# Two decode attentions on one core: the small input first, a memset in pieces, and a last weight load in shrinking parts

## Chip, cores and metric

The kernel runs on one core of one Trainium2 chip. The metric is the device time of one execution in microseconds (us), median over runs. The span in a profile (first to last instruction) is 1.7 to 2.2 us shorter than the time of the same run.

## The reference, cut to what matters

Two independent one-token attentions, A and B, with 32 query heads, 16 key/value heads, head size 128, model width 576. A looks at the last 2048 cache rows, B at all 8192. All data are bf16.

```python
q = (x @ wq).reshape(...)                 # x: 576 numbers, wq: 576 x 4096
p = softmax((q @ k.T) * 128**-0.5)        # per head
y = (p @ v).reshape(4096) @ wo            # wo: 4096 x 576
# the result is concat(y_A, y_B)
```

About 103 MB must come from HBM, and each byte is used once.

## The kernel before

A small scheduler takes operations with the tiles they read and write, derives the semaphore waits and emits one program per engine. SyncE ("sp") issues all big loads into six 2 MB slots, reused in turn. These parts matter here:

```python
def setup(pool):                       # GpSimd zeroes small tiles, among them xpad
    ...
for b in range(2):                     # then the two halves of ptm, 32 KB per partition each
    add("pool", lambda pool, b=b: pool.memset(ptm[:, b, :].bitcast(U32), 0), writes=[("ptm", b)])

def setup2(pool):                      # four more memsets, without a wait between them
    pool.memset(identf[:], 0.0); pool.memset(pick[:], 0.0)
    pool.memset(same[:], 0.0);   return pool.memset(opj[:], 0.0)
# ... then affine_selects, each of which waits for the memset of its tile

add("act", lambda act: act.activation(warm[:, 4:8], warm[:, 0:4], ACT.Exp), ...)
load_x(0); load_x(1)                   # on ACT: 128 runs of 10 bytes each, after the activation

def x_columns(P):                      # VectorE: two tiny tensor_scalars, x into xpad
    for e in range(2):
        add("dve", lambda dve, e=e: dve.tensor_scalar(xpad[:, P, 5*e:5*e+5, 0], xtwo[:, P, 0:5],
                                                      par[2][:, e:e+1], None, ALU.mult), ...)
# the q projection (TensorE, "PE") needs xpad and wq; its end frees the slots of wq

def load_wo(P, k):                     # wo in three loads: 14, 14 and 4 rows per partition
    lo, hi = k * WO_SLOT, min(HQ, (k + 1) * WO_SLOT)
    ...
def wo_part(P, k, s):                  # four matmuls a row; waits for its whole load
    ...
for k in range(3):                     # the last work of the kernel
    wo_part(1, k, load_wo(1, k))
finish_out(1); store_out(1)            # copy of PSUM, store
```

A "row" of wo is 1,152 bytes in each of the 128 partitions. wo has 32 of them.

Of the kernel before, what the change touches and what calls it, by code (L numbers as in the profile page):

```python
# [6 lines left out]
U32 = mybir.dt.uint32  # L7
# [4 lines left out]
HQ = 32  # L12
HKV = 16
DH = 128
DM = 576
# [4 lines left out]
NSLOT = 6  # L20
# [1 line left out]
TS = 64  # L22
WQ_UNITS = 9
WQ_SLOT = 4
WO_SLOT = 14
OUTW = DM // 4


# [9 lines left out]
class Program:  # L38
# [11 lines left out]
        self.dma_sems = {}  # L50
        self.dma_count = {}

    def add(self, eng, fn, reads=(), writes=(), dma=None):
        op = Op(eng, fn, tuple(reads), tuple(writes), dma)
        deps = []
        for r in op.reads:
            w = self.writer.get(r)
            if w is not None:
                deps.append((w, True))
            if r[0] == "bank":  # L60
                deps += [(o, False) for o in self.readers.get(r, ())]
        for r in op.writes:
            w = self.writer.get(r)
            if w is not None:
                deps.append((w, False))
            deps += [(o, False) for o in self.readers.get(r, ())]
        for r in op.reads:
            self.readers.setdefault(r, []).append(op)
        for r in op.writes:
            self.writer[r] = op  # L70
            self.readers[r] = []
        for o, raw in deps:
            if o is op:
                continue
            if o.dma_sem is None and o.eng == eng and (not raw or eng in ("pe", "sp")):
                continue
            op.deps.append(o)
            o.needed = True
        if dma is not None:
            if dma not in self.dma_sems:  # L80
                self.dma_sems[dma] = self.nc.alloc_semaphore("dma_" + dma)
                self.dma_count[dma] = 0
            self.dma_count[dma] += 16
            op.value = self.dma_count[dma]
        self.ops.append(op)
        return op
# [50 lines left out]
def bass_concat_heads__sliding_block_cached__gqa_block_cached__decode_kernel(  # L137
# [13 lines left out]
    xs = [A_x, B_x]  # L151
# [3 lines left out]
    wos = [A_wo, B_wo]  # L155
# [14 lines left out]
    add = prog.add  # L170

    slots = nc.alloc_sbuf_tensor("slots", [128, NSLOT, SLOT], BF16)
    kt = nc.alloc_sbuf_tensor("kt", [128, NKT, UNIT], BF16)
    ptm = nc.alloc_sbuf_tensor("ptm", [128, 2, 32 * 512], BF16)
# [8 lines left out]
    xtwo = nc.alloc_sbuf_tensor("xtwo", [128, 2, 8], BF16)  # L183
# [6 lines left out]
    opj = nc.alloc_sbuf_tensor("opj", [128, 2, 64], BF16)  # L190
# [11 lines left out]
    B_M = ("bank", 7)  # L202


    def setup(pool):
        def zero(t):
            return pool.memset(t, 0.0)
        zero(ident[:])
        zero(xpad[:])
        zero(selq[:])  # L210
        pool.memset(onesf[:], 1.0)
        zero(warm[:])
        return zero(qtm[:])

    add("pool", setup, writes=["ident", ("xpad", 0), ("xpad", 1), "selq", "ones", "warm", ("qtm", 0), ("qtm", 1)])

    def select(t, base_, pattern, mult):
        return lambda pool: pool.affine_select(out=t, in_=t, compare_op=ALU.not_equal, fill=1.0,
                                               base=base_, pattern=pattern, channel_multiplier=mult)

    add("pool", select(ident[:], 0, [[-1, 128]], 1), reads=["ident"], writes=["ident"])
    add("pool", select(selq[:], 0, [[-32, 4]], 1), reads=["selq"], writes=["selq"])
    for b in range(2):
        add("pool", lambda pool, b=b: pool.memset(ptm[:, b, :].bitcast(U32), 0), writes=[("ptm", b)])  # L224

    def setup2(pool):
        pool.memset(identf[:], 0.0)
# [11 lines left out]
    for n in (2, 4):  # L239
        add("dve", lambda dve, n=n: dve.tensor_reduce(par[n][:, :], ident[:, :].rearrange("p (m g) -> p g m", g=n),  # L240
                                                      AX.X, ALU.add),
            reads=["ident"], writes=[("par", n)])
# [4 lines left out]
    slot_n = [0]  # L247

    def load(src_of, view_of, what):
        s = slot_n[0] % NSLOT  # L250
        slot_n[0] += 1
        res = ("slot", s)
        add("sp", lambda sp: sp.dma_start(view_of(slots[:, s, :]), src_of()), writes=[res], dma="slot%d" % s)
        return s


    def load_x(P):
        def go(act):
            x = xs[P]
            with nc.allow_non_contiguous_dma(reason="small x load"):  # L260
                src = bass.AP(tensor=x.tensor, offset=x.offset, ap=[[9, 64], [4, 2], [1, 5]])
                return act.dma_start(xtwo[:, P, 0:5], src)
        add("act", go, writes=[("xtwo", P)], dma="x%d" % P)

    def load_wq(P, k):
        lo, hi = k * WQ_SLOT * 2048, min(WQ_UNITS, (k + 1) * WQ_SLOT) * 2048
        return load(lambda: wqs[P].rearrange("(m r) n -> m (r n)", m=64)
                    .rearrange("m (e y) -> (m e) y", e=2)[:, lo:hi],
                    lambda v: v[:, 0:hi - lo], "wq")
# [6 lines left out]
            return a[0, i * G[P]:(i + 1) * G[P], r0:r0 + CH[P], :].rearrange("g (p t) d -> p g (t d)", t=TS)  # L276
        return load(src, lambda v: v, "kv")

    def load_wo(P, k):
        lo, hi = k * WO_SLOT, min(HQ, (k + 1) * WO_SLOT)  # L280
        return load(lambda: wos[P].rearrange("(p j) n -> p (j n)", p=128)[:, lo * DM:hi * DM],
                    lambda v: v[:, 0:(hi - lo) * DM], "wo")


    def x_columns(P):
# [188 lines left out]
    def combine(P):  # L474
        n = NCH[P]
        last = n - 1
        d = 2
        add("dve", lambda dve: dve.tensor_scalar(acc[:, d, :], opsum[:, 0:DH], st(P, C_AL + last), None, ALU.mult),  # L478
            reads=[B_O, ("st", P, C_AL)], writes=[("acc", d)])
        for c in range(last):  # L480
            add("dve", lambda dve, c=c: dve.scalar_tensor_tensor(acc[:, d, :], acc[:, c, :], st(P, C_AL + c),
                                                                 acc[:, d, :], ALU.mult, ALU.add),
                reads=[("acc", c), ("acc", d), ("st", P, C_AL)], writes=[("acc", d)])

        def mm(pe):
            for r in range(4):
                ins = pe.matmul(misc[:, 0:32], lhsT=pick[:, r, :], rhs=acc[:, d, 32 * r:32 * r + 32],
                                start=(r == 0), stop=(r == 3))
            return ins
        add("pe", mm, reads=["pick", ("acc", d)], writes=[B_M])  # L490
        add("dve", lambda dve: dve.tensor_copy(opj[:, P, 0:32], misc[:, 0:32]), reads=[B_M], writes=[("opj", P)])

    def wo_part(P, k, s):
        lo, hi = k * WO_SLOT, min(HQ, (k + 1) * WO_SLOT)

        def mm(pe):
            for jj in range(lo, hi):
                for j in range(4):
                    o = (jj - lo) * DM + j * OUTW
                    ins = pe.matmul(misc[32 * j:32 * j + 32, 0:OUTW], lhsT=opj[:, P, jj:jj + 32],  # L500
                                    rhs=slots[:, s, o:o + OUTW], start=(jj == 0), stop=(jj == HQ - 1))
            return ins
        add("pe", mm, reads=[("opj", P), ("slot", s)], writes=[B_M])

    def finish_out(P):
        add("dve", lambda dve: dve.tensor_copy(outsb[:, P, :], misc[:, 0:OUTW]), reads=[B_M], writes=[("outsb", P)])
# [5 lines left out]
            return eng.dma_start(dst, src)  # L512
        add("sp", put, reads=[("outsb", P)], writes=[("out", P)], dma="out%d" % P)


    load_x(0)
    load_x(1)

    def k_phase(P, c, between):
        pend = None  # L520
# [39 lines left out]
    n = 64 * NS[0]  # L560
# [12 lines left out]
    v_keep(1, 0)  # L573
    softmax_transpose(1, 1, pb1)
    weights(1)
    for k in range(3):
        wo_part(0, k, load_wo(0, k))
    finish_out(0)
    vb1 = list(range(NS[1]))
    v_some(1, 1, vb1, NS[1])  # L580
    store_out(0)
    combine(1)
    for k in range(3):
        wo_part(1, k, load_wo(1, k))
    finish_out(1)
    store_out(1)
    add("sp", lambda sp: sp.nop(), reads=[("out", 0), ("out", 1)])
# [29 lines left out]
```

## Time and profile before

| kernel before | |
|---|---|
| time, median | 254.84 us (254.61 to 255.10, 4 runs) |
| span of the profiled run | 252.8 us |
| moved by DMA | 103.24 MB |
| first packet of a big load | 1.74 us |
| last landing of wo of B | 249.30 us |
| end of PE's last matmul | 250.30 us |

First the page of the kernel before: the span in 40 slices of 6.3 us. A digit is the busy share in tenths, and GB/s is what the DMA engines moved.

```profile
PE   0018999787799995888694994858943634332563
DMA  7999999999999999999999999999999999999960
GB/s 283 398 440 430 433 415 428 433 417 425 432 423 423 430 423 423 433 421 423 430 417 436 425 415 436 430 412 441 421 421 419 430 425 425 428 423 429 425 284 31
```

The DMA engines are full from the second slice to the last two; PE is full only here and there. 103.24 MB at 425 GB/s take 243 us. Only what lies before the first packet and after the engines begin to run dry can change the time.

Next its chain of waits, with start, length and what was waited for. Two stretches matter, the head and the tail:

```profile
2.54 9.25 DMA xtwo<-in_A_x_dram
11.79 0.03 issue
11.81 6.05 DVE xpad L287 x2
...
219.21 28.70 DMA slots<-in_B_wo_dram
247.91 0.04 issue
247.95 2.38 PE misc L500 x60
```

The head waits 9.25 us for 1.2 KB of x, then 6.05 us for two VectorE operations on 5 elements per partition. The timeline of the kernel before (start, length, engine, line, operation) shows what GpSimd (POOL) did meanwhile:

```profile
3.12 13.79 POOL L224 MEMSET ptm<- 128x8192 uint32 x2
...
17.61 0.21 POOL L230 MEMSET opj<- 128x128 bf16 x1
17.96 0.29 POOL L218 TENSOR_SCALAR_AFFINE_SELECT identf<-identf 128x128 f32<-128x128 f32 x1
```

And this is the timeline of the tail before:

```profile
243.44 1.87 PE L500 MATMUL misc<-slots,opj 128*32 128x144 bf16 x56 [0.37 <-DVE opj L491]
247.95 2.35 PE L500 MATMUL misc<-slots,opj 128*32 128x144 bf16 x72 [2.64 <-DMA slots<-in_B_wo_dram]
250.36 0.31 DVE L506 CAST outsb<-misc 128x144 bf16<-128x144 f32 x1 [7.06 <-PE misc L500]
```

PE waits for a whole 14-row load, and then has 72 matmuls (18 rows) to do at the very end. They ran at a granted TensorE clock (the share of full speed that the throttle allowed) of 0.50, 33 ns each.

One more reading comes from the landing records. Each load has sixteen landing records, read here as one for each of the sixteen DMA engines. For the last load of the kernel before these landings are, in us:

```
242.83 242.84 242.90 243.00 243.05 243.43 243.71 244.14 | 247.35 247.37 247.42 247.46 247.56 247.63 249.06 249.30
```

Eight engines are done 3 to 6.5 us before the other eight. PE starts on a load only after its sixteenth landing (at 247.95 us after a last landing at 247.91), so the slowest engine sets the end.

### The profile page before, as it was taken

How to read it: one execution, taken by the hardware profiler on the slowest of the kernel's cores; microseconds unless marked ns; L12 is line 12 of the kernel's file. 1: busy time of each engine (PE TensorE's matmuls, PEld its weight loads, DVE VectorE, ACT ScalarE, POOL GpSimd, SP SyncE). 2: the span in 40 equal slices, each digit the busy share in tenths (PEclk: the TensorE clock that was granted, in tenths of full speed). 3: DMA queues.
4: the chain of work that ended last, by engine and by line, in shares of the span. 5: the costliest groups of instructions: out<-in, count | busy, mean ns of one | idle time of the engine just before them, and what ended most of it. 6: DMA issues, size and time to landing. Idle time of an engine off the chain costs nothing.

```text
span 252.8 us, 7319 instructions
## 1 busy us (share of the span) xinstructions
PE 167.1 (66%) x3438; PEld 131.7 (52%) x3438; DVE 79.3 (31%) x141; ACT 87.3 (35%) x92; POOL 22.4 (9%) x31
## 2 busy tenths in 40 slices
PE   0018999787799995888694994858943634332563
PEld 0003877456578874766474673655732633232453
DVE  0181545427544462357341340313425100000010
ACT  2000766445566683565461461423630000000000
POOL 8996000000000000000000000000000000000000
PEclk9999999999979999799997798968977665555555
DMA  7999999999999999999999999999999999999960
GB/s 283 398 440 430 433 415 428 433 417 425 432 423 423 430 423 423 433 421 423 430 417 436 425 415 436 430 412 441 421 421 419 430 425 425 428 423 429 425 284 31
DMA packets 7822, 103.24 MB, mean 408 GB/s; under 512 B 1136, under 2 KB 1136, under 8 KB 1648
## 3 DMA queue, kind: packets, MB, share of 16 engines
q1 hardware_dynamic: 7504, 102.77, 96.1%
q8 instruction: 27, 0.44, 0.7%
q10 hardware_dynamic: 288, 0.00, 0.1%
q14 instruction: 3, 0.02, 0.0%
HBM read 102.76 MB, written 0.00 MB: 407 GB/s over the span
## 4 chain that ended last, share of the span: by engine, by line
DMA 53%; PE 38%; DVE 6%; issue 1%; POOL 1%; ACT 0%; SPq 0%; POOLq 0%
DMA slots<-in_B_k_cache_dram 21%; PE ktps L339 20%; DMA slots<-in_B_v_cache_dram 17%; DMA slots<-in_B_wo_dram 11%; PE sacc L362 7%; DMA xtwo<-in_A_x_dram 4%; PE opsum L464 3%; DVE xpad L287 3%; PE opsum L302 2%; PE misc L302 2%; PE misc L500 2%; DVE ptm L407 1%; PE misc L396 1%; PE misc L444 1%; PE misc L431 0%
## 5 line engine op out<-in xcount | busy, mean ns | idle before, releaser
L345 ACT ACTIVATE kt<-ktps 128x1024 bf16<-128x1024 bf16 x80 | 78.0, 1023 | 65.3 <-PE ktps L339 65.1
L339 PE MATMUL ktps<-ident,slots 128*128 128x128 bf16 x1280 | 86.4, 231 | 19.1 <-DMA slots<-in_B_k_cache_dram 19.1
L339 PEld LDWEIGHTS ktps<-ident,slots 128*128 128x128 bf16 x1280 | 80.0, 105 | 31.5 <-DMA slots<-in_B_k_cache_dram 20.3
L348 DVE COPY kt<-ktps 128x1024 bf16<-128x1024 bf16 x80 | 55.3, 691 | 79.2 <-PE ktps L339 79.0
L464 PE MATMUL opsum<-slots,ptm 128*32 128x128 bf16 x1280 | 28.3, 256 | 29.4 <-DMA slots<-in_B_v_cache_dram 28.9
L464 PEld LDWEIGHTS opsum<-slots,ptm 128*32 128x32 bf16 x1280 | 24.5, 116 | 35.6 <-DMA slots<-in_B_v_cache_dram 33.0
L362 PE MATMUL sacc<-kt,qtm 128*32 128x512 bf16 (+1 forms) x384 | 30.1, 411 | 0.3 <-DVE kt L348 0.3
L302 PE MATMUL opsum<-slots,xpad 128*32 128x512 bf16 x72 | 8.7, 460 | 19.3 <-DVE xpad L287 19.3
L302 PEld LDWEIGHTS opsum<-slots,xpad 128*32 128x32 bf16 x72 | 2.5, 112 | 22.2 <-issue 21.3
L224 POOL MEMSET ptm<- 128x8192 uint32 x2 | 13.8, 6926 | 0.0
L478 DVE TENSOR_SCALAR acc<-opsum,stat 128x128 f32<-128x128 f32 x2 | 0.7, 346 | 39.6 <-PE opsum L464 39.6
L362 PEld LDWEIGHTS sacc<-kt,qtm 128*32 128x32 bf16 x384 | 7.0, 98 | 6.9 <-ACT kt L345 1.1
L500 PE MATMUL misc<-slots,opj 128*32 128x144 bf16 x256 | 8.1, 323 | 3.4 <-DMA slots<-in_B_wo_dram 2.6
L308 ACT ACTIVATE qrow<-opsum 128x512 bf16<-128x512 f32 x2 | 1.2, 597 | 24.1 <-PE misc L302 24.1
L500 PEld LDWEIGHTS misc<-slots,opj 128*32 128x32 bf16 x256 | 7.4, 146 | 3.8 <-DMA slots<-in_B_wo_dram 3.4
L287 DVE TENSOR_SCALAR xpad<-xtwo,par 128x5 bf16<-128x5 bf16 x4 | 6.4, 3098 | 8.3 <-DMA xtwo<-in_A_x_dram 8.3
L302 PE MATMUL misc<-slots,xpad 128*32 128x512 bf16 x72 | 8.5, 450 | 0.0
L385 ACT ACTIVATE psb<-sacc,stat 128x2048 bf16<-128x2048 f32 x3 | 5.9, 1967 | 7.5 <-DVE stat L379 7.5
L562 POOL MEMSET ptm<- 128x512 uint32 x1 | 0.5, 526 | 86.1 <-PE opsum L464 86.1
L407 DVE TENSOR_SCALAR ptm<-misc,par 128x256 bf16<-128x256 bf16 (+1 forms) x16 | 6.9, 526 | 3.7 <-PE misc L396 3.7
L396 PE MATMUL misc<-ident,psb 128*128 128x128 bf16 x48 | 4.1, 235 | 3.7 <-DVE ptm L407 3.7
L396 PEld LDWEIGHTS misc<-ident,psb 128*128 128x128 bf16 x48 | 3.0, 105 | 5.4 <-DVE ptm L407 4.3
(50 smaller groups left out, 37.2 us busy)
## 6 DMA issues: line engine op xcount, KB each, us to landing
slots<-in_B_k_cache_dram SPq DMA_DIRECT2D x16, 2048.0 KB, 22.3
slots<-in_B_v_cache_dram SPq DMA_DIRECT2D x16, 2048.0 KB, 25.1
slots<-in_A_k_cache_dram SPq DMA_DIRECT2D x4, 2048.0 KB, 19.3
slots<-in_A_v_cache_dram SPq DMA_DIRECT2D x4, 2048.0 KB, 20.7
slots<-in_A_wq_dram SPq DMA_DIRECT2D x2, 2048.0 KB, 9.6
slots<-in_B_wq_dram SPq DMA_DIRECT2D x2, 2048.0 KB, 18.6
slots<-in_A_wo_dram SPq DMA_DIRECT2D x2, 2016.0 KB, 25.0
slots<-in_B_wo_dram SPq DMA_DIRECT2D x2, 2016.0 KB, 28.7
```

The lines of the kernel that those rows point to most:

```text
L224: add("pool", lambda pool, b=b: pool.memset(ptm[:, b, :].bitcast(U32), 0), writes=[("ptm", b)])
L287: add("dve", lambda dve, e=e: dve.tensor_scalar(xpad[:, P, 5 * e:5 * e + 5, 0], xtwo[:, P, 0:5], par[2][:, e:e + 1], None, ALU.mult), read ...
L302: ins = pe.matmul(qps[c][32 * j:32 * j + 32, :], lhsT=xpad[:, P, x, :], rhs=slots[:, s, o:o + 512], start=(u == 0), stop=(u == WQ_UNITS - 1))
L339: ins = pe.matmul(ktps_bf[q][:, t * 128:(t + 1) * 128], lhsT=slots[:, s, o:o + 128], rhs=ident[:, :], start=True, stop=True, is_transpose= ...
L345: add("act", lambda act, q=q, dst=dst: act.activation(dst, ktps_bf[q], ACT.Copy), reads=[("bank", q)], writes=[("kt", u, q)])
L348: add("dve", lambda dve, q=q, dst=dst: dve.tensor_copy(dst, ktps_bf[q]), reads=[("bank", q)], writes=[("kt", u, q)])
L362: ins = pe.matmul(sacc[32 * j:32 * j + 32, o:o + w], lhsT=qtm[:, P, g * 32:(g + 1) * 32], rhs=rhs, start=(g == 0 and o % 512 == 0), stop=( ...
L385: return act.activation(psb[:, 0:w * G[P]].rearrange("p (x g) -> p x g", g=G[P]), src, ACT.Exp, bias=st(P, C_NB + c), scale=SCALE, accum_o ...
L396: ins = pe.matmul(misc_bf[:, t * 128:(t + 1) * 128], lhsT=psb[:, o:o + 128], rhs=ident[:, :], start=True, stop=True, is_transpose=True)
L407: ins = dve.tensor_scalar(dst, src, par[G[P]][:, e:e + 1], None, ALU.mult)
L464: ins = pe.matmul(opsum[32 * j:32 * j + 32, 0:DH], lhsT=ptm[:, pb, o:o + 32], rhs=slots[:, s, b * 128:(b + 1) * 128], start=(i == 0 and u ...
L500: ins = pe.matmul(misc[32 * j:32 * j + 32, 0:OUTW], lhsT=opj[:, P, jj:jj + 32], rhs=slots[:, s, o:o + OUTW], start=(jj == 0), stop=(jj == ...
```

## The change

The intent: let x arrive before the big loads, let VectorE in between the pieces of the memset, and give PE less to do after the last bytes arrive.

```diff
+    load_x(0)                      # now first in ACT's program
+    load_x(1)
     def setup(pool):
...
     for b in range(2):
-        add("pool", lambda pool, b=b: pool.memset(ptm[:, b, :].bitcast(U32), 0), writes=[("ptm", b)])
+        for h in range(8):
+            add("pool", lambda pool, b=b, h=h: pool.memset(ptm[:, b, h * 2048:(h + 1) * 2048].bitcast(U32), 0),
+                writes=[("ptm", b)])
...
-    def load_wo(P, k):             # one load for one slot
+    def load_wo(P, lo, parts):     # one slot, several loads, a semaphore for each part
...
-    for k in range(3):
-        wo_part(1, k, load_wo(1, k))
+    for lo, parts in ((0, [14]), (14, [8, 4]), (26, [3, 2, 1])):
+        for made in load_wo(1, lo, parts):
+            wo_part(1, *made)
```

wo of A keeps its loads of 14, 14 and 4 rows.

More of the change, by code (lines that the diff above doesn't have):

```diff
@@ L24 @@
 WQ_SLOT = 4
-WO_SLOT = 14
 OUTW = DM // 4
@@ L51, in __init__, with add @@
         self.dma_count = {}
-    def add(self, eng, fn, reads=(), writes=(), dma=None):
+    def add(self, eng, fn, reads=(), writes=(), dma=None, after=()):
         op = Op(eng, fn, tuple(reads), tuple(writes), dma)
@@ L61, in add @@
                 deps += [(o, False) for o in self.readers.get(r, ())]
+        for r in after:
+            deps += [(o, False) for o in self.readers.get(r, ())]
         for r in op.writes:
@@ L202, in bass_concat_heads__sliding_block_cached__gqa_block_cached__decode_kernel, with load_x, go @@
     B_M = ("bank", 7)
+    def load_x(P):
+        def go(act):
+            x = xs[P]
+            with nc.allow_non_contiguous_dma(reason="small x load"):
+                src = bass.AP(tensor=x.tensor, offset=x.offset, ap=[[9, 64], [4, 2], [1, 5]])
+                return act.dma_start(xtwo[:, P, 0:5], src)
+        add("act", go, writes=[("xtwo", P)], dma="x%d" % P)
+    load_x(0)
+    load_x(1)
     def setup(pool):
@@ L254, in load @@
         return s
-    def load_x(P):
-        def go(act):
-            x = xs[P]
-            with nc.allow_non_contiguous_dma(reason="small x load"):
-                src = bass.AP(tensor=x.tensor, offset=x.offset, ap=[[9, 64], [4, 2], [1, 5]])
-                return act.dma_start(xtwo[:, P, 0:5], src)
-        add("act", go, writes=[("xtwo", P)], dma="x%d" % P)
     def load_wq(P, k):
@@ L277, in load_kv, with go @@
         return load(src, lambda v: v, "kv")
-    def load_wo(P, k):
-        lo, hi = k * WO_SLOT, min(HQ, (k + 1) * WO_SLOT)
-        return load(lambda: wos[P].rearrange("(p j) n -> p (j n)", p=128)[:, lo * DM:hi * DM],
-                    lambda v: v[:, 0:(hi - lo) * DM], "wo")
+    def load_wo(P, lo, parts):
+        s = slot_n[0] % NSLOT
+        slot_n[0] += 1
+        o, made = 0, []
+        for k, rows in enumerate(parts):
+            n = rows * DM
+            res = ("slot", s) if len(parts) == 1 else ("slot", s, k)
+            def go(sp, lo=lo, n=n, o=o):
+                return sp.dma_start(slots[:, s, o:o + n],
+                                    wos[P].rearrange("(p j) n -> p (j n)", p=128)[:, lo * DM:lo * DM + n])
+            add("sp", go, writes=[res], after=[("slot", s)], dma="slot%d" % s if res == ("slot", s) else "part%d_%d" % (s, k))
+            made.append((lo, lo + rows, s, o, res))
+            lo += rows
+            o += n
+        return made
     def x_columns(P):
@@ L491, in combine, with wo_part @@
         add("dve", lambda dve: dve.tensor_copy(opj[:, P, 0:32], misc[:, 0:32]), reads=[B_M], writes=[("opj", P)])
-    def wo_part(P, k, s):
-        lo, hi = k * WO_SLOT, min(HQ, (k + 1) * WO_SLOT)
+    def wo_part(P, lo, hi, s, o0, res):
         def mm(pe):
@@ L498, in mm @@
                 for j in range(4):
-                    o = (jj - lo) * DM + j * OUTW
+                    o = o0 + (jj - lo) * DM + j * OUTW
                     ins = pe.matmul(misc[32 * j:32 * j + 32, 0:OUTW], lhsT=opj[:, P, jj:jj + 32],
@@ L502, in mm @@
             return ins
-        add("pe", mm, reads=[("opj", P), ("slot", s)], writes=[B_M])
+        add("pe", mm, reads=[("opj", P), res], writes=[B_M])
     def finish_out(P):
@@ L513, in store_out @@
         add("sp", put, reads=[("outsb", P)], writes=[("out", P)], dma="out%d" % P)
-    load_x(0)
-    load_x(1)
     def k_phase(P, c, between):
@@ L575, in bass_concat_heads__sliding_block_cached__gqa_block_cached__decode_kernel @@
     weights(1)
-    for k in range(3):
-        wo_part(0, k, load_wo(0, k))
+    for lo, parts in ((0, [14]), (14, [14]), (28, [4])):
+        for made in load_wo(0, lo, parts):
+            wo_part(0, *made)
     finish_out(0)
@@ L582, in bass_concat_heads__sliding_block_cached__gqa_block_cached__decode_kernel @@
     combine(1)
-    for k in range(3):
-        wo_part(1, k, load_wo(1, k))
+    for lo, parts in ((0, [14]), (14, [8, 4]), (26, [3, 2, 1])):
+        for made in load_wo(1, lo, parts):
+            wo_part(1, *made)
     finish_out(1)
```

## The prediction

One sentence of the recorded text is cut where the mark stands. The 0.9 us are my estimate from the 6.93 us of the memset, and rest on the idea that VectorE's wait ends with one GpSimd instruction. The trace before did not show that: the wait ended at 17.86 us, and the memset at 16.91.

> What bounds the kernel now. The DMA engines, from 2 us to the end. The page's DMA row is 9 in all slices but the first and the last two; 103.24 MB at about 425 GB/s are 243 us of the 252.8 us span. The single packet records agree: between 2 and 242 us about 16.1 packets are in flight on 16 engines, without a gap. PE (66%), ACT and DVE have slack. Only the head (first packet at 1.7 us) and the tail can give anything back.
>
> The head. The chain of waits starts with the x load: issued at 2.54 us behind the first ACTIVATE, landed at 11.79. Its first packet moves at 6.65 us, when the first wq load's eight packets per engine are through, and then one small packet passes per 0.61 us wq packet. Then the two tensor_scalars into xpad take 6.03 us; the same ones for B take 0.23. They end when the second ptm memset (6.93 us, until 16.9) is over. [...] With memsets of about 0.9 us (an eighth of 6.93, plus start-up) DVE should wait 0.9 us or less, and an early x should land at 3 to 7 us. The q projection then begins when wq lands, near 8 us, instead of 18.0, and ends near 16.5 instead of 24.4. That frees about 8 us of PE time, but not on the limiting path: loads of 10.5 MB (25 us) are queued at 4 us, and the fourth K slot, issued at 21.7, kept the queue full. I expect about 0 from it. One risk: ACT and SP now both issue at 0.73 us, and an x issue takes 0.59; the whole stream may start up to 0.5 us later.
>
> The tail. The engines don't finish together. Of B's second wo load the first engine is done at 241.4, the last at 247.91; of the third, 242.8 and 249.30. Each instruction fetch (16 KB, about 1.05 us) sets one engine back by about 1.5 us. Bytes and PE instructions stay, so this skew stays. Now PE waits until 247.95 for 14 rows, then runs 72 matmuls (18 rows) in 2.35 us, to 250.3; a row costs 0.13 us of PE and 0.345 us of the slowest engine. With 8, 4, 3, 2, 1 rows PE follows the arrivals and has one row left after the last landing. Extra: 24 packets per engine at about 8 ns (16,128 B take 604 ns, 4,608 B take 178) and three completions of 9 ns: 0.2 us. So last landing 249.5, PE end about 249.9 (one row plus some 0.3 us of latency) instead of 250.3. Copy and store stay.
>
> Sum: -0.4 us in the tail, 0 from the head, up to +0.5 at risk at the start: 254.5 us, range 253.5 to 255.4. Chances: faster by over 2% 0.01, within 2% 0.98, slower 0.01.
>
> Shown right by: q matmuls starting near 8 us, xpad ops under 1 us each; DMA row full as before; fourth K issue near 10 us; last wo landing 249.3 to 249.7; after it 4 to 12 matmuls. Shown wrong by: x landing after 11 us; first wq packet later than 2 us; the last landing moved by over 0.5 us.
>
> What would make it wrong: instruction fetches falling on other engines (1.5 us either way), dearer small packets, or a stream at another rate when PE is 8 us ahead.

## The result

| | before | after |
|---|---|---|
| time, median | 254.84 us (4 runs) | 254.60 us (254.14 to 254.81, 4 runs) |
| ratio to before | | 0.9988 (0.9971 to 1.0005) |
| x of A issued, landed | 2.54, 11.79 us | 0.73, 10.66 us |
| xpad operations end | 17.86 us | 18.41 us |
| fourth K load of A issued | 21.71 us | 21.92 us |
| last landing of wo of B | 249.30 us | 249.18 us |
| PE's last matmul ends | 250.30 us | 249.47 us |

A ratio is the mean time of one kernel's fast runs over that of the other's in the same rounds, so it is not quite the ratio of the medians. The difference is not clear of noise: the interval holds 1.

The page of after, the same rows:

```profile
PE   0008999787799995888893784956934535333573
DMA  7999999999999999999999999999999999999971
GB/s 273 400 450 418 431 431 407 433 431 423 420 434 423 421 434 418 423 434 420 423 431 426 418 431 429 423 418 439 423 422 423 428 423 429 426 426 425 415 309 56
```

The DMA row is as full as before. The head in the chain of waits of after:

```profile
0.73 9.93 DMA xtwo<-in_A_x_dram
10.68 7.74 DVE xpad L306 x2
```

The issue moved up by 1.8 us, but the landing only by 1.1. The two VectorE operations take longer than before. The timeline of after says why:

```profile
0.73 0.59 ACTq L211 DMA_DIRECT2D xtwo<-in_A_x_dram  x1
0.73 1.33 SPq L268 DMA_DIRECT2D slots<-in_A_wq_dram  x3
...
3.12 14.35 POOL L238 MEMSET ptm<- 128x1024 uint32 x16
...
18.16 0.20 POOL L245 MEMSET opj<- 128x128 bf16 x1
18.51 0.29 POOL L231 TENSOR_SCALAR_AFFINE_SELECT identf<-identf 128x128 f32<-128x128 f32 x1
```

ACT and SyncE issue in the same instant. The sixteen memset pieces run back to back: in their single records each starts about 0.06 us before the one ahead of it ends. When x lands, eight of them and four more memsets are still to end. VectorE finishes at 18.41 us, in the first gap of GpSimd (18.37 to 18.51). Before it was the same: it finished at 17.86, in the gap from 17.82 to 17.96, and not when the ptm memset ended at 16.91.

The tail of after:

```profile
245.68 1.10 PE L517 MATMUL misc<-slots,opj 128*32 128x144 bf16 x32 [0.60 <-DMA slots<-in_B_wo_dram]
247.09 0.43 PE L517 MATMUL misc<-slots,opj 128*32 128x144 bf16 x16 [0.30 <-DMA slots<-in_B_wo_dram]
248.16 0.37 PE L517 MATMUL misc<-slots,opj 128*32 128x144 bf16 x12 [0.63 <-DMA slots<-in_B_wo_dram]
248.86 0.61 PE L517 MATMUL misc<-slots,opj 128*32 128x144 bf16 x12 [0.33 <-DMA slots<-in_B_wo_dram]
249.52 0.31 DVE L523 CAST outsb<-misc 128x144 bf16<-128x144 f32 x1 [6.46 <-PE misc L517]
```

PE follows the arrivals, and four matmuls start after the last landing at 249.18 us. PE ends 0.83 us earlier than before, yet the span is only 0.50 us shorter (252.78 to 252.28). The missing 0.33 us lie in the closing barrier: GpSimd's last two records are 0.08 us apart before, and 0.42 us after.

So three theories were to be tested. Tail: the split loads give what there is to gain. Head: it is off the limiting path, whether quick or slow. Lock (the name here for VectorE's waits of 6.05 and 7.74 us while GpSimd runs): VectorE gets in only where GpSimd pauses. The rivals are written with each run.

### The profile page after: what moved, and what is told of

Its sections match the earlier page's. It is cut to its first block, busy times and chain, and to the rows that moved or that the text cites. A ratio compares the mean times of both kernels' runs of the same rounds, so it can differ in the third digit from the quotient of the medians.

```text
span 252.3 us, 7334 instructions
## 1 busy us (share of the span) xinstructions
PE 165.5 (66%) x3438; PEld 129.3 (51%) x3438; DVE 81.0 (32%) x141; ACT 87.2 (35%) x92; POOL 22.9 (9%) x45
## 4 chain that ended last, share of the span: by engine, by line
DMA 61%; PE 29%; DVE 6%; issue 1%; ACT 0%; SPq 0%
DMA slots<-in_B_k_cache_dram 21%; DMA slots<-in_B_v_cache_dram 19%; PE ktps L358 15%; DMA slots<-in_B_wo_dram 10%; DMA slots<-in_A_v_cache_dram 8%; PE sacc L381 5%; DMA xtwo<-in_A_x_dram 4%; DVE xpad L306 3%; PE opsum L483 2%; PE opsum L321 2%; PE misc L321 2%; PE misc L517 2%; DVE ptm L426 1%; PE misc L415 1%; PE misc L463 1%
## 5 line engine op out<-in xcount | busy, mean ns | idle before, releaser
L358 PE MATMUL ktps<-ident,slots 128*128 128x128 bf16 x1280 | 85.3, 230 | 19.6 <-DMA slots<-in_B_k_cache_dram 19.6
L358 PEld LDWEIGHTS ktps<-ident,slots 128*128 128x128 bf16 x1280 | 78.8, 104 | 32.7 <-DMA slots<-in_B_k_cache_dram 20.8
L381 PE MATMUL sacc<-kt,qtm 128*32 128x512 bf16 (+1 forms) x384 | 30.8, 418 | 0.3 <-DVE kt L367 0.3
L321 PE MATMUL opsum<-slots,xpad 128*32 128x512 bf16 x72 | 8.1, 427 | 19.9 <-DVE xpad L306 19.9
L238 POOL MEMSET ptm<- 128x1024 uint32 x16 | 14.3, 951 | 0.0
L306 DVE TENSOR_SCALAR xpad<-xtwo,par 128x5 bf16<-128x5 bf16 x4 | 8.1, 3941 | 7.1 <-DMA xtwo<-in_A_x_dram 7.1
L517 PEld LDWEIGHTS misc<-slots,opj 128*32 128x32 bf16 x256 | 6.7, 135 | 3.9 <-DMA slots<-in_B_wo_dram 3.5
```

The costliest lines, as they stand in the source:

```text
L238: add("pool", lambda pool, b=b, h=h: pool.memset(ptm[:, b, h * 2048:(h + 1) * 2048].bitcast(U32), 0), writes=[("ptm", b)])
L306: add("dve", lambda dve, e=e: dve.tensor_scalar(xpad[:, P, 5 * e:5 * e + 5, 0], xtwo[:, P, 0:5], par[2][:, e:e + 1], None, ALU.mult), read ...
L321: ins = pe.matmul(qps[c][32 * j:32 * j + 32, :], lhsT=xpad[:, P, x, :], rhs=slots[:, s, o:o + 512], start=(u == 0), stop=(u == WQ_UNITS - 1))
L358: ins = pe.matmul(ktps_bf[q][:, t * 128:(t + 1) * 128], lhsT=slots[:, s, o:o + 128], rhs=ident[:, :], start=True, stop=True, is_transpose= ...
L381: ins = pe.matmul(sacc[32 * j:32 * j + 32, o:o + w], lhsT=qtm[:, P, g * 32:(g + 1) * 32], rhs=rhs, start=(g == 0 and o % 512 == 0), stop=( ...
L517: ins = pe.matmul(misc[32 * j:32 * j + 32, 0:OUTW], lhsT=opj[:, P, jj:jj + 32], rhs=slots[:, s, o:o + OUTW], start=(jj == 0), stop=(jj == ...
```

## The experiments

Ratios are to the kernel before, in the rounds of the same job. One per mille is 0.25 us. Each edit is made to after unless it says otherwise.

### The tail alone, the head alone

e1_tail_only is the kernel before with the split tail loads; e2_head_only is after with the old tail:

```diff
# e2
-    for lo, parts in ((0, [14]), (14, [8, 4]), (26, [3, 2, 1])):
+    for lo, parts in ((0, [14]), (14, [14]), (28, [4])):
# e1, from after: load_x back behind ACT's activation, and
-        for h in range(8):
-            add("pool", ... ptm[:, b, h * 2048:(h + 1) * 2048] ...)
+        add("pool", ... ptm[:, b, :] ...)
```

> The kernel before with the split tail loads alone (x late, memsets whole). My theory (the gain is all in the tail): faster than before by 0.3 to 0.6 us (ratio 0.998 to 0.999), PE's last matmul of wo ends within 0.5 us of the last wo landing, the head as before (first q matmul near 18.0 us). Rival (the gain came from the head): 254.8 us, no difference to before.

Measured: 254.55 us, ratio 0.9991 (0.9978 to 1.0003). The first q matmul starts at 18.00 us as before, and PE ends 0.36 us after the last landing. The sign fits the tail theory, but the interval reaches past 1. In this trace the last landing fell at 250.04 us.

> After without the split tail loads: x first and sixteen memset pieces alone. My theory: the same as before within 0.2 us; PE runs 72 wo matmuls after the landing of the 14 rows, as before. x lands near 10.6 us, the two xpad ops end near 18.4 us. Rival (the head is on the limiting path): slower than before by about the 0.55 us that the q projection starts later, or faster if early x counts.

Measured: 255.33 us, ratio 1.0022 (1.0008 to 1.0035): slower than before by 0.55 us, 0.2 to 0.9. I had expected no difference, and the rival about this much. But the rival's reason is not what the trace shows. The DMA engines are as full as before and the last landing, 249.42 us, is 0.12 us later than before. After the store is issued it takes 2.43 us to the end instead of 2.08, which is the barrier. The barrier is 0.34 us of the loss; the 0.12 us of the landing is less than it moves between runs, and the rest of the 0.55 is within the interval.

### Pauses between the pieces

```diff
-                writes=[("ptm", b)])
+                reads=[("ptm", b)], writes=[("ptm", b)])     # each piece waits for the one before
```

> After, but each memset piece waits for the one before (a semaphore wait on GpSimd between pieces). Theory on the lock: VectorE gets in at the first pause of GpSimd, not at the first end of an instruction, so now the xpad ops take under 1.2 us each, end by 12 us, and the q projection starts by 12 us instead of 18.5. Rival (VectorE is held off by GpSimd's whole work, or by something else): the xpad ops still end at 18 us or later. Theory on the limit (head off the limiting path): time equal to after within 0.3 us although the q projection ends 6 us earlier. Rival: up to 6 us faster.

Timeline of e3:

```profile
10.80 0.38 DVE L306 TENSOR_SCALAR xpad<-xtwo,par 128x5 bf16<-128x5 bf16 x2 [7.26 <-DMA xtwo<-in_A_x_dram]
...
11.32 0.62 PE L321 MATMUL opsum<-slots,xpad 128*32 128x512 bf16 x4 [11.32 <-DVE xpad L306]
```

Measured: 254.66 us, ratio 0.9998 (0.9986 to 1.0011). Both theories stand. With pauses VectorE is through in 0.38 us instead of 7.74, the pieces being the same. And q starting 7.2 us earlier, with the fourth K load issued at 15.03 us instead of 21.92, gains nothing.

### x ahead of everything

```diff
# e3, and
-        add("act", go, writes=[("xtwo", P)], dma="x%d" % P)
+        add("sp" if P == 0 else "act", go, writes=[("xtwo", P)], dma="x%d" % P)
```

> e3 with the x load of A issued on SyncE ahead of the wq loads, in their queue. Theory: x lands before 5 us since no wq packet is ahead of it; xpad is done by 6 us; the q projection starts when wq lands, 8 to 9.5 us. The stream of big loads starts 0.6 us later (one x issue), so the time is 0.5 to 0.8 us over e3's. If the x packets themselves hold the wq packets up, by more: 2 to 4 us. Rival (the head limits): faster than before by over 2 us.

Timeline of e6:

```profile
3.46 0.65 DVE L306 TENSOR_SCALAR xpad<-xtwo,par 128x5 bf16<-128x5 bf16 x2
9.85 0.11 PEld L321 LDWEIGHTS opsum<-slots,xpad 128*32 128x32 bf16 x4 [9.85 <-DMA slots<-in_A_wq_dram]
```

Measured: 255.54 us, ratio 1.0033 (1.0020 to 1.0045), 0.9 us over e3, a little more than expected. x of A landed at 3.12 us. x of B, still issued on ACT, landed at 2.88 instead of e3's 13.93: I read this as the big packets ahead holding x up, and not the queue it was issued on. q now waits for wq alone and starts at 9.85 us. The first big packet starts at 2.89 us instead of 1.76 in e3, and by 12 us 3.53 MB have moved instead of 3.96, which is 1.0 us at 425 GB/s. That is about the whole loss. I had counted one x issue (0.67 us here), and the first big packet is 1.13 us later; that the small packets keep the big ones waiting for the rest is my reading. Such is the head that the change was after, and it makes the kernel slower: what delays the first big packet costs, and what delays q within its reserve does not.

### How much the head may be late

```diff
# e4: the xpad operations of A also wait for a GpSimd tile that is ready near 21.8 us
-                reads=[("xtwo", P), ("par", 2)], writes=[("xpad", P)])
+                reads=[("xtwo", P), ("par", 2)] + (["pick"] if P == 0 else []), writes=[("xpad", P)])
# e5: for a later one ("same"), whose loop now runs four times
-    for dj in range(-3, 4):
+    for dj in list(range(-3, 4)) * 4:
```

> After with the xpad ops of A waiting for GpSimd's pick tile, so the q projection starts about 3.3 us later (near 21.9 us). Theory: the fourth K load of A is issued near 25.3 us and still ahead of the end of the queued loads (29.1 us), so time equal to after within 0.3 us. Rival (head on the limiting path): 3 us slower.

Measured: 255.16 us, ratio 1.0013 (0.9989 to 1.0038). q began 3.84 us later. The interval (-0.3 to +1.0 us) rules out the rival's 3 us, but it is too wide to say whether the delay is free. The single packets show 0.15 us of DMA time lost between 24 and 32 us, so this delay is already at the edge of the reserve.

> After with the xpad ops waiting for the same tile, whose loop runs four times, so the q projection starts about 15 us later (near 33.5 us). Theory: the loads in flight run dry at 29.1 us, the fourth K load of A is issued near 37 us; the DMA engines stand idle for 8 to 10 us there and the time grows by 8 to 10 us, less than the 15 us of the delay. Rival (head on the limiting path all along): 15 us slower. Rival (head never counts): equal.

Busy times by stretch, e5: the last three columns are the granted clock, the DMA share and GB/s.

```profile
24.00:32.00 8.00, 0.00 (x0) 0.00 (x0) 0.00 (x0) 0.00 (x0) 5.40 (x19) 1.00 0.53 226
32.00:40.00 8.00, 5.63 (x60) 2.49 (x64) 0.37 (x2) 0.00 (x0) 1.17 (x4) 1.00 0.09 33
```

The same stretches of after:

```profile
24.00:32.00 8.00, 7.19 (x128) 6.19 (x132) 4.75 (x9) 6.00 (x7) 0.44 (x2) 1.00 1.01 426
32.00:40.00 8.00, 8.00 (x136) 6.02 (x129) 3.61 (x6) 5.08 (x6) 0.00 (x0) 1.00 1.00 422
```

Measured: 265.76 us, ratio 1.0430 (1.0407 to 1.0452), 11 us more. q began at 34.37 us, 15.8 us later than in after. The lost DMA time is 8 x (1.01 - 0.53) + 8 x (1.00 - 0.09) = 11.1 us, and that is the whole loss. So the head has about 15.8 - 11.1 = 4.7 us of reserve in after, if beyond it each microsecond costs one. That slope was not measured by itself; from e4 (3.84 us late, 0.15 us lost) to e5 (15.8 late, 11.1 lost) it is 0.92. I had expected 8 to 10 us, as I had put the refill 1 us too early.

### The big load last

```diff
-    for lo, parts in ((0, [14]), (14, [8, 4]), (26, [3, 2, 1])):
+    for lo, parts in ((0, [4]), (4, [14]), (18, [14])):
```

> After with wo of B in loads of 4, 14 and 14 rows, the big one last. Theory: the last landing stays at 249.1 to 249.4 us, and PE has 56 matmuls (1.85 us) left after it: PE ends near 251.2 us, 0.8 us later than before and 1.7 later than after; time 0.6 to 1.0 us over before. Rival (order and size of the last load don't count): equal to before.

Timeline of e7:

```profile
249.34 1.87 PE L517 MATMUL misc<-slots,opj 128*32 128x144 bf16 x56 [2.76 <-DMA slots<-in_B_wo_dram]
251.26 0.31 DVE L523 CAST outsb<-misc 128x144 bf16<-128x144 f32 x1 [8.07 <-PE misc L517]
```

Measured: 255.99 us, ratio 1.0052 (1.0037 to 1.0067), 1.3 us over before. Last landing 249.30 us, PE ends at 251.21 us as expected. This is the clearest support of the tail theory: what PE has left after the last landing is paid in full. PE ends 0.9 us later than before; another 0.33 us is the barrier, which e7 shares with after, and which I had left out of the expectation.

### The barrier and the number of GpSimd instructions

```diff
-        for h in range(8):
-            add("pool", ... ptm[:, b, h * 2048:(h + 1) * 2048] ...)
+        for h in range(4):
+            add("pool", ... ptm[:, b, h * 4096:(h + 1) * 4096] ...)
```

> After with four memset pieces for each half instead of eight: 61 GpSimd records instead of 69 (before 55). In every trace with 69 the last two barrier records of GpSimd are 0.41 to 0.43 us apart, in those with 55 and with 111 0.08. Theory (the place of GpSimd's last instructions in its program costs this, so their count does): 0.08 us, the end 0.34 us earlier after the store than in after, time about 0.3 us under after. Rival (splitting the memset as such does it): 0.42 us and equal to after. Theory on the lock: pieces back to back let VectorE in at none of their ends, so the xpad ops still end at about 18 us.

GpSimd's records, and the distance of its last two, both in the closing barrier:

| kernel | GpSimd records | distance |
|---|---|---|
| before, e1 | 55 | 0.08 us |
| e11 | 61 | 0.08 us |
| after, e2, e3, e4, e6, e7, e8, e9, e10, e13 | 69 | 0.41 to 0.43 us |
| e5 | 111 | 0.08 us |

Measured: 254.46 us, ratio 0.9991 (0.9977 to 1.0005). The step in the trace is as expected: it goes with the number of instructions and not with the splitting, since e11 and e5 have split memsets and no step. That the cause is the place of the last instructions in the program is only argued. One more sign of it: the ten traces with the step have an instruction fetch of 8 KB 0.6 to 0.9 us after their last record, and the four without it have none. In the times 0.33 us can't be told from noise here, and e11 had less to gain than expected: the time outside its span is 2.02 to 2.17 us in its five runs, against 1.81 to 1.94 us in after's and 1.75 to 1.81 us in those of before in e11's job. Most of what e11 saves inside the span it thus pays outside it, for a reason that these traces don't show. VectorE ended at 18.08 us after 7.47 us (7.73 in after), so bigger pieces change little about its wait.

### Giving the early engines more

After's last landings span 242.94 to 249.18 us. Moving bytes from the late to the early eight engines might save 2 us. Two tries:

```diff
# e9, the last six rows: the source seen as 8 x 16 rows
+                    src = bass.AP(tensor=wo.tensor, offset=wo.offset + lo * DM,
+                                  ap=[[16 * HQ * DM, 8], [HQ * DM, 16], [1, n]])
# e10, six rows as sixteen loads of eight partitions
+                    return [sp.dma_start(slots[p:p + 8, s, o:o + n], wo[p:p + 8, :]) for p in range(0, 128, 8)]
-    for lo, parts in ((0, [14]), (14, [8, 4]), (26, [3, 2, 1])):
+    for lo, parts in ((0, [14]), (14, [6, 6]), (26, [3, 2, 1])):
```

> After with the last six rows (loads of 3, 2, 1) moved by eight DMA engines instead of sixteen (source with an outer dim of 8). In after one half of the engines ends near 244, the other at 247.6 to 249.2. If the eight engines used here are the early half: the late half ends 2.07 us earlier (six rows at 0.345 us), the early half at 246.4, last landing near 247.1 and time 2 us under after. If they are the late half: last landing near 251.3 us and time 2 us over after. If the loads still run on sixteen engines: equal.

Measured: 254.45 us, ratio 0.9991 (0.9977 to 1.0005). The landings were those of after (242.96 to 249.32), with sixteen spread landings for each load: the loads still ran on sixteen engines. The try says nothing about the idea.

> After with six of B's last 18 wo rows moved by sixteen loads of eight partitions each, which I expect to run on eight engines only; the small store of A (four partitions, four landings) landed with the early half of the engines in every trace, so I take these eight to be the early half. Theory (the tail is the skew between the halves): the late half ends six rows times 0.345 us = 2.07 us earlier, near 247.1 us, the early half near 246.4; time 1.7 to 2.2 us under after, 252.4 to 252.9 us. Rival (these are the late engines): 2 us slower. Rival (the loads spread over all sixteen): equal to after, within 0.3 us, less or plus the cost of small packets.

Busy times by stretch, e10:

```profile
240.00:244.00 4.00, 3.08 (x68) 2.81 (x56) 0.70 (x2) 0.00 (x0) 0.00 (x0) 0.50 0.95 212
244.00:248.00 4.00, 0.87 (x22) 0.73 (x26) 0.19 (x1) 0.00 (x0) 0.00 (x0) 0.50 0.87 254
```

The same in after:

```profile
240.00:244.00 4.00, 2.71 (x37) 2.60 (x40) 0.90 (x3) 0.00 (x0) 0.00 (x0) 0.50 0.85 342
244.00:248.00 4.00, 2.62 (x86) 1.89 (x76) 0.00 (x0) 0.00 (x0) 0.00 (x0) 0.67 0.46 182
```

Measured: 260.84 us, ratio 1.0236 (1.0222 to 1.0250). The engines are busy (0.95) and move less than in after (212 GB/s against 342). The loads did run on eight engines: the sixteen loads have 128 landings, besides one record each at issue. The first landing, at 236.9 us, follows the first engine's end of the load ahead (236.4 us), so early engines were among them. But not all eight were early, as the expectation has it. Two engines of the early half landed the load behind the sixteen at 240.3 us, too soon to have moved a share of them (16 packets of at least 262 ns, 4.2 us). So at least two of the eight were late engines, and the idea was not put to the test. Nor does that explain the whole loss, as the packets became slow.

The sixteen loads moved 885 KB (16 x 8 x 6,912 B) from 236.9 to 251.4 us, 61 GB/s, and the 6,912-byte packets took up to 516 ns (median over 2 us) against 262 ns at the end. The other loads slowed down as well: packets of 16,128 B, which belong to the load ahead, rose from 604 ns to 1,100 to 1,144 ns (medians over 2 us, 238 to 244 us), and the late engines ended that load at 244.6 to 247.5 us instead of 241.3 to 242.9. What made the packets slow was not shown, as no run separated one cause from another.

### What sets the late half back

The prediction said that each instruction fetch of 16 KB sets one engine back by about 1.5 us. Before and after have 27 such fetches each, of 1.06 and 1.07 us in the mean. In before the spread of a load's sixteen landings grows from 0.46 to 1.94 us around the 1st fetch, and from 4.96 to 6.51 us around the 25th. Two tries to add fetches:

```diff
# e8, behind each V slot
+        def idle(pe):
+            for _ in range(128 if P == 0 else 96):
+                ins = pe.nop()
+            return ins
+        add("pe", idle)
# e13, in the same place
+        def more(pe):
+            for _ in range(64 if P == 0 else 48):
+                ins = pe.matmul(misc[:, 0:128], lhsT=ident[:, :], rhs=ident[:, :], start=True, stop=True)
+            return ins
+        add("pe", more, reads=["ident"], writes=[B_M])
```

> After with 2048 empty PE instructions (128 behind each of A's four V slots, 96 behind each of B's sixteen), 8 more fetches of 16 KB. Theory (each fetch sets one of eight engines back by about 1.5 us, in turn; the end is set by the engine hit most often): with 34 instead of 26 fetches before the end the most-hit engine is hit five times instead of four; spread of the last landings 7.4 to 8 us instead of 6.2, last landing and time 1.2 to 1.6 us later, provided that PE still keeps up with the loads. Rival (fetches are not what sets the late half back): spread and time as in after.

Measured: 254.66 us, ratio 0.9997 (0.9982 to 1.0011). The trace has 27 fetches and as many PE records as after: the empty instructions left no trace of themselves. The try is void.

> The repeat of the fetch test, since the empty instructions of the last try left no record: after with 1024 useless matmuls (64 behind each of A's four V slots, 48 behind each of B's sixteen; with their weight loads 2048 PE records more, so 8 more fetches of 16 KB, 35 instead of 27). Theory (each fetch sets one of eight engines back by about 1.5 us, in turn; the end is set by the engine hit most often): the DMA row stays full, the spread of the last landings grows from 6.2 to between 7.4 and 8 us, last landing and time 1.2 to 1.6 us later than after. Rival (fetches are not what sets the late half back): spread near 6.2 us and time as in after.

Measured: 263.23 us, ratio 1.0328 (1.0305 to 1.0350), far over both expectations. The proviso failed: PE did not keep up. All 128 wo matmuls came after the last landing (250.86 us), so the time does not decide between the theories. The landings do. The table gives, around the 9th, 17th and 25th fetch, its start and the distance of first and last landing of a load just before and just after:

| fetch | after: start, spread | e13: start, spread |
|---|---|---|
| 9th | 91.7 us, 1.95 to 3.19 us | 93.7 us, 2.04 to 3.48 us |
| 17th | 156.2 us, 3.54 to 4.74 us | 146.0 us, 3.64 to 5.05 us |
| 25th | 231.2 us, 5.06 to 6.40 us | 195.7 us, 5.18 to 6.43 us |

The spread grows by a step at the same fetch and not at the same time: the 25th came 35 us earlier in e13, and so did the step. The 1st fetch fits too (in after, from 0.43 to 1.68 us). Fetches 2 to 8 after each step move one more engine to the late end and leave the spread nearly alone. That is the pattern of fetches that go round eight engines and cost each 1.2 to 1.5 us. After 214 us the count no longer holds: the spread fell to 4.13 us, by my reading because PE's lag left the engines without loads and they drew level in part; the 33rd fetch, at 247.7 us, brings the step once more (4.24 to 5.66 us).

What held PE up is in the waits of e13 (engine, tile, what it waited for, total, times, longest; "issue" means that it waited for nothing the profile shows):

```profile
PE opsum L483 <- issue: 9.0, 8, 2.0
PE misc L492 <- issue: 6.6, 6, 1.7
PE misc L523 <- issue: 2.1, 1, 2.1
```

In after the same line waits for loads, and on "issue" only once, for 0.5 us:

```profile
PE opsum L483 <- DMA slots<-in_B_v_cache_dram: 29.2, 10, 4.3
```

In e13 the fetches follow each other mostly every 6 to 7 us from 100 us on, and the late gaps (near 242.9, 248.9 and 254.5 us) lie within some 2 us of a fetch's start (241.7, 247.7, 253.6). That PE waited for instructions there is my reading, and not shown by a run that removes it.

### No better version

The lowest median is e9's, 254.45 us, beside 254.61 us for before in its job; after, e1, e9 and e11 are all at ratios of 0.9988 to 0.9991, with intervals that hold 1. No version beats both kernels clear of noise.

## Why the prediction was right, and where it was not

The time was predicted at 254.5 us, 253.5 to 255.4, and measured at 254.60. The structure was right: DMA-bound from 2 us on, head worth nothing, tail worth a few tenths. The time alone could not have shown it: the stated range also holds the 254.84 us of before, so a change that does nothing would have fallen into it as well. The traces and the experiments carry the account. Point by point:

- **The head is off the limiting path: right.** After itself could not test this, as its q starts 0.55 us later than before and not 10 us earlier. e3 starts q 7.2 us earlier and gains nothing. e5 shows the limit of it: about 4.7 us of reserve, then nearly one for one.
- **"an early x should land at 3 to 7 us": wrong.** It landed at 10.66. ACT and SyncE issue at the same moment, and the first x packet moves only at 5.39 us, 4.7 us after its issue (before: at 6.65, 4.1 us after). I had read the wait before as the wq packets in line ahead, and then assumed that simultaneous issue would be ahead of them. In e6, where x was ahead, it landed 2.4 us after its issue.
- **"With memsets of about 0.9 us ... DVE should wait 0.9 us or less": wrong.** The pieces took 0.95 us each, and VectorE took 7.7 us. I had also read the end of the wait before wrongly, as the end of the second ptm memset; it was the first pause of GpSimd, four memsets later. That the wait ends with one GpSimd instruction was not shown: in after VectorE waited through twelve back-to-back memsets, and in e3, with a pause after each piece, it took 0.38 us.
- **q near 8 us, fourth K issue near 10 us: wrong** for these two reasons (18.55 and 21.92 us).
- **The tail, -0.4 us: right as a mean over traces.** PE ended at 249.47 us in after's trace, 0.83 us earlier than before. But last landings move between runs: in the six traces with the split tail and no other delay (after, e1, e3, e8, e9, e11; e4 and e6, which delay the loads, have 250.27 and 250.34) they are at 249.18 to 250.04 us, mean 249.59, and PE ends at 249.93 us in the mean; in the two traces with the old tail (before, e2) PE ends at 250.36. That is 0.43 us, with the last landing at 249.59 where I had put 249.5 and the end where I had put 249.9.
- **"Copy and store stay": they did (0.31 and 0.57 us), but the barrier behind them, which the prediction left out, took 0.33 us more.** Within the span it takes back most of the tail's gain: -0.43 + 0.33 = -0.1 us. The measured change is -0.3 us with an interval from -0.74 to +0.13.
- **The risk of a later start did not come true.** The first big packet moves at 1.74 us in both.

So the prediction was right in the sum, and with some luck. Both steps that it had wrong in the head did not count, because the head does not count within its reserve. The omitted barrier was small against the range, but nearly as large as the gain that was forecast.

## What to carry to other kernels

Before mending a slow stretch, ask whether the bounding resource is starved by it: here 9 us of waiting for x and 6 us of VectorE's wait beside GpSimd cost nothing that the times show, while 1.1 us of delay to the first big load cost 0.9 us. When a stream of loads bounds a kernel, shrink what must be computed after the last landing, and expect as the gain only that remainder less the extra packets (here 0.43 us at the end of PE, as a mean over traces). Splitting GpSimd's memset did not let VectorE in earlier (7.74 us); pauses between the pieces did (0.38 us).
